# Attention and two gated layers on one core: the sixth head pair's reciprocals taken from the summed rows on VectorE, and two chunks' scores in one TensorE visit in the first stretch

## The chip, the cores and the metric

The kernel runs on one core of one Trainium2 chip. The metric is the device time of the program in microseconds (us); the time of a kernel is the median of its runs. TensorE does the matmuls, VectorE, ScalarE and GpSimd the work between them, and SP issues most of the DMAs. In the rows the engines are PE, DVE, ACT and POOL.

## The reference

Attention over 4 batches, 12 heads, 448 positions and 64 columns a head, with capped scores, followed by two feed-forward layers over the 1792 tokens of 768 columns. All is float32.

```python
scores = scale * np.matmul(q, k.transpose(0, 1, 3, 2))
scores = cap * np.tanh(scores / cap)
attn = np.exp(scores - max); attn = attn / (sum(attn) + 1e-09)
x = np.matmul(attn, v)
h = np.maximum(np.maximum(x @ w1, x @ w2), x @ w3) @ w_out
out = (silu(h @ w_gate) * (h @ w_val)) @ moe2_w_out
```

The lines are shortened; the feed-forward weights come in as 64-bit floats and are made into 32-bit ones on the chip.

## The kernel before, in words

**Pairs and chunks.** Two heads make a pair, six pairs a batch; g counts the 24 pairs from 0, so that the sixth pair is g = 5. The keys of a pair are cut into four chunks; chunk n belongs to pair n // 4. The first three chunks of a pair hold 128 keys of either head, the fourth holds the last 64 keys of both. For a chunk, `scores(n)` makes the products of keys and queries in PSUM (for the first three chunks two matmuls of 64 rows side by side, three times over, since each factor is held in two parts), `tanhs(n)` and `exps(n)` are ScalarE's tanh and exp, and `values(n)` adds the chunk's products with the values. The cap bounds the scores, so the exponent needs no maximum from the data. For pairs g < 8 (`PLAIN`) the values and exponentials are plain float32; from g = 8 on `parts(n)` cuts the exponentials into two parts, `eh` on ScalarE and `el` on VectorE (L286).

**The sums.** The values stand in a tile of three columns of blocks: the first head's values, a block of ones, the second head's values. The matmul of the first head takes the first two blocks, that of the second head the last two. So the sum of the exponentials comes out along with the products, once on each of 64 rows: below the products for the first head, above them for the second.

**From the sums to x.** `take(g)` copies the two PSUM tiles to `o`: the first head's by VectorE, with one row of sums (65 rows), the second head's by ScalarE, with all 128 rows. `sums_out(g)` loads a row of sums of each head by DMA into 112 rows of 8 (`su`), `invert(g)` takes the reciprocals there, `inverse_out(g)` stores them to memory (`rd`), `spread(g)` loads them back on 64 rows for each head (`rb`). `finish(g)` multiplies `o` by `rb` into `xp` (two multiplies, L366), and makes the two parts of `x` (L368, L369). In the first stretch `finish` is GpSimd's, but the sixth pair's is VectorE's. The tile `xp` has one buffer (L361), `e`, which holds tanh and exp, four (L267), the PSUM of the scores two, one for even and one for odd chunks (L257). The sums' PSUM of the second head has one buffer; for the first head it alternates between two in the first stretch (L179).

**The order of the work.** Everything runs in the order in which it is written out, engine by engine. `slot(n)` lists the steps around chunk n, with c = n % 4. The first stretch is the loop over n from -6 to 31 (L783), with `alone` set: there are no feed-forward matmuls yet. In slot n it does the exp of chunk n+1, the scores of chunk n+3, the tanh of chunk n+2 and the products of chunk n. In c = 0 the pair before is taken, with the second head's copy behind the tanh. Between the slots stand steps that make the feed-forward weights into 32-bit floats: `one`, `clamp` and `two` on VectorE (L609 to L624), `four` on GpSimd (L627), and `split_next`, which cuts a weight into two parts with ScalarE and GpSimd (L639 to L642), behind slots 27 and 30. Behind the stretch `alone` is cleared (L796), and the later slots are woven with the matmuls of the first feed-forward layer (`ff1`, L699). Slots of that part already do two chunks' scores in one visit: in c = 1 the chunks n+3 and n+4, in c = 2 none.

**The sixth pair.** Its sums are taken in slot 24 and sent off in slot 25, its reciprocals follow in slot 28, `rb` is loaded in slot 29, and VectorE finishes it in slot 31, behind that slot's `parts(32)` and `prep_k(9)`, which makes `kh9` and `kl9`. The fifth pair's `finish` stands in slot 28 on GpSimd.

Of the kernel before, what the change touches and what calls it, by code (L numbers as in the profile page):

```python
# [9 lines left out]
F32 = mybir.dt.float32  # L10
# [113 lines left out]
def program(ctx, tc, tensors, shared, general):  # L124

    nc = tc.nc
# [5 lines left out]
    B, H, S, D = q.shape  # L132
    P = 128
# [3 lines left out]
    NK = DM // P  # L137
# [181 lines left out]
    def take(g, heads=(0, 1)):  # L319

        if 0 in heads:
            if g < PLAIN:
                o[g] = res.tile([P, 2, S], F32, tag="x", name=f"o{g}", bufs=2 * NK)
            else:
                o[g] = ring.tile([P, 2, S], F32, tag="o", name=f"o{g}")
        for j in heads:
            r = slice(0, D + 1 if j == 0 else P)
            src, dst = pv[g][j][r, :S], o[g][r, j]
            if alone and j == 0:
                nc.vector.tensor_copy(dst, src)  # L330
            else:
                nc.scalar.activation(dst, src, AF.Copy)
# [17 lines left out]
    def spread(g):  # L350
        if g < NP:
            rb[g] = res.tile([P, 2, S], F32, tag="x", name=f"rb{g}", bufs=2 * NK)[:, 0]
        else:
            rb[g] = ring.tile([P, S], F32, tag="rb", name=f"rb{g}", bufs=1)
        for j in range(2):
            nc.sync.dma_start(
                out=rb[g][j * D : (j + 1) * D], in_=rd[g % 2][j].partition_broadcast(D)
            )

    def finish(g, eng=None):  # L360
# [42 lines left out]
    def slot(n):  # L403
# [5 lines left out]
        def add(cost, fn, i, end, *args):  # L409
            if 0 <= i < end:  # L410
                steps.append((cost, lambda: fn(i, *args)))
# [18 lines left out]
                    add(0, inverse_out, n // 4 - 2, NPAIR)  # L430
        add(0, exps, n + 1, NG)
        add(0, parts, n + 1, NG)
        together = c == 3 and not alone

        def products(i):
            if 0 <= i < NG:
                values(i)

        ahead = [n + 3] if alone else [[n + 3], [n + 3, n + 4], [], [n + 3]][c]

        def next_scores():
            for i in ahead:
# [4 lines left out]

        if ahead:
            steps.append((len(ahead) + together, next_scores))
        for i in [n + 2] if alone else ahead:  # L450
            add(0, tanhs, i, NG)
        if c == 0 and alone:
            add(0, take, n // 4 - 1, NPAIR, (1,))
            add(0, finish, n // 4 - 3, NPAIR)
            add(0, invert, n // 4 - 2, NPAIR)
            if n // 4 - 2 == NP - 1:
                add(0, inverse_out, NP - 1, NPAIR)
        if alone and n == -6:
            add(0, prep_q, 0, NPAIR)
        if n == 4 * PLAIN - 3:  # L460
            add(0, prep_v, PLAIN, NPAIR)
        if c == 1:
            add(0, sums_out, n // 4 - 1, NPAIR)
            if alone and n // 4 - 2 != NP - 1:
                add(0, inverse_out, n // 4 - 2, NPAIR)
            else:
                add(0, spread, n // 4 - 2, NPAIR)
            add(0, prep_q, (n + 7) // 4, NPAIR)
        if c == 2:
            if n > -4:  # L470
                add(0, load_k, n // 4 + 3, NPAIR)
            if alone and n // 4 - 2 != NP - 1:
                add(0, spread, n // 4 - 2, NPAIR)
            if not alone:
                add(0, prep_k, (n + 6) // 4, NPAIR)
                add(0, invert, n // 4 - 1, NPAIR)
                add(0, finish, n // 4 - 2, NPAIR)
        if c == 3:
            if alone:
                add(0, prep_k, (n + 5) // 4, NPAIR)  # L480
                if n // 4 - 2 == NP - 1:
                    add(0, finish, NP - 1, NPAIR, nc.vector)
            if not alone:
                add(0, inverse_out, n // 4 - 1, NPAIR)
            add(0, load_q, n // 4 + 4, NPAIR)
# [271 lines left out]
    with tc.manual_schedule():  # L757
# [22 lines left out]
        else:  # L780
            load_v(0)
            left = 4 * 10
            for n in range(-6, 4 * NP + FIRST):  # L783
# [8 lines left out]
                    ones(1)  # L792
                if n in (4 * NP + 3, 4 * NP + 6):
                    split_next()
            tanhs(4 * NP + FIRST + 2)
        alone.clear()  # L796
        for b in range(B - 1):
            if general:
# [502 lines left out]
```

## Time and profile before

| | us |
|---|---|
| median of 3 runs | 1048.73 (1047.07 to 1049.38) |
| the profiled execution, its own time | 1047.95 |
| its span, first to last instruction | 1046.2 |
| TensorE busy | 1026.9 (98%) |
| VectorE busy | 812.7 (78%) |
| ScalarE busy | 534.6 (51%) |
| GpSimd busy | 614.4 (59%) |
| chain that ended last, on TensorE | 83% |

Busy times are sums over the instructions of an engine. Matmuls are pipelined, so a busy TensorE need not be at its peak. The chain that ended last is followed back from the last instruction, at each step to what released it. A wait is put down to the event that came last. All times in the rows are us from the start of the span.

### The profile page before, as it was taken

To read this page: it belongs to the slowest core of one execution; us is meant where nothing else is said; L and a number is where in the kernel's file an instruction comes from. 1 tells how busy PE (TensorE), PEld (TensorE's weight loads), DVE (VectorE), ACT (ScalarE), POOL (GpSimd) and SP (SyncE) were. 2 spreads that over 40 slices of the span, in tenths; PEclk is the share of its full clock that TensorE was granted. 3 is DMA by queue.
4 is the path that set the end of the run, shared out by engine and by line. 5 is a ranking of instruction groups with operands and counts; after the bars stand their busy time and mean duration, and the time that the engine had idled before them with its cause. 6 is when DMAs were issued, how large, how long until landed. Compare 5 with 4: busy or idle time off the path is not lost.

```text
span 1046.2 us, 15070 instructions
## 1 busy us (share of the span) xinstructions
PE 1026.9 (98%) x5348; PEld 912.8 (87%) x5348; DVE 812.7 (78%) x1076; ACT 534.6 (51%) x843; POOL 614.4 (59%) x524
## 2 busy tenths in 40 slices
PE   8999999999999999999999999999999999999997
PEld 5555877888888888999999999999999999999997
DVE  5898889879889787877366977888887777986763
ACT  6887777767677764344445533333333334643331
POOL 2479977599999999999311356556666662000000
PEclk9999999999999999999999999999999999999999
DMA  7866344424435323434322023445544338765311
GB/s 179 205 165 169 78 125 130 130 64 136 120 105 145 107 83 108 144 105 140 96 83 87 1 61 122 156 158 167 169 161 135 96 112 254 210 181 147 103 46 41
DMA packets 153653, 131.42 MB, mean 126 GB/s; under 512 B 71136, under 2 KB 144096, under 8 KB 153568
## 3 DMA queue, kind: packets, MB, share of 16 engines
q1 hardware_dynamic: 147552, 108.67, 35.4%
q0 software_dynamic: 4944, 21.46, 6.5%
q8 instruction: 44, 0.72, 0.3%
q10 hardware_dynamic: 1072, 0.23, 0.1%
q14 instruction: 41, 0.34, 0.1%
HBM read 98.70 MB, written 31.54 MB: 124 GB/s over the span
## 4 chain that ended last, share of the span: by engine, by line
PE 83%; DVE 6%; POOL 5%; DMA 3%; issue 2%; ACT 2%; SPq 0%; ACTq 0%; POOLq 0%; DVEq 0%
PE ps_g L1036 29%; PE ps_h L699 19%; PE ps_o L1174 15%; PE ps_y L699 8%; PE pv L311 7%; PE sc L262 4%; DVE el L286 2%; POOL ws L642 2%; DVE xp L366 1%; PE pq L228 1%; DMA rb<-rd 1%; DMA vp<-in_v_dram 1%; POOL w L627 1%; POOL xp L366 1%; PE pk L242 1%
## 5 line engine op out<-in xcount | busy, mean ns | idle before, releaser
L699 PE MATMUL ps_h<-x,ws 128*128 128x448 f32 x1296 | 279.9, 366 | 3.4 <-POOL ws L642 3.4
L699 PEld LDWEIGHTS ps_h<-x,ws 128*128 128x128 f32 x1296 | 240.5, 188 | 30.2 <-issue 7.8
L642 POOL TENSOR_TENSOR ws<-w,ws 128x384 fp32r<-128x384 f32 x144 | 184.2, 1288 | 13.3 <-ACT ws L639 5.4
L627 POOL TENSOR_TENSOR t<-t,raw 128x768 uint32<-128x768 uint32 x42 | 82.6, 1967 | 113.9 <-DVE raw L624 107.1
L286 DVE TENSOR_TENSOR el<-e,eh 128x896 fp32r<-128x896 f32 x64 | 92.9, 1452 | 28.9 <-ACT eh L285 27.6
L276 ACT ACTIVATE e<-e,four 128x896 f32<-128x896 f32 x96 | 99.6, 1037 | 0.8
L1036 PE MATMUL ps_g<-yo,o_S 128*128 128x448 f32 x432 | 93.5, 362 | 0.0
L268 ACT ACTIVATE e<-sc,four 128x896 f32<-128x896 f32 x96 | 85.5, 905 | 13.3 <-PE sc L262 11.9
L699 PE MATMUL ps_y<-ha,ws 128*128 128x448 f32 x432 | 87.5, 364 | 0.0
L699 PEld LDWEIGHTS ps_y<-ha,ws 128*128 128x128 f32 x432 | 81.0, 188 | 6.3
L1036 PEld LDWEIGHTS ps_g<-yo,o_S 128*128 128x128 f32 x432 | 81.0, 187 | 5.4
L613 ACT ACTIVATE t<-raw 128x768 f32<-128x768 f32 x50 | 45.1, 903 | 65.5 <-DMA raw<-in_moe_w_val_dram 31.2
L311 PE MATMUL pv<-eh,vs 128*128 128x448 f32 (+1 forms) x256 | 77.5, 373 | 0.0
L641 POOL TENSOR_SCALAR ws<-w 128x384 fp32r<-128x384 f32 x90 | 71.7, 797 | 0.4
L1036 PE MATMUL ps_g<-yo,o_A 128*128 128x448 f32 x324 | 70.3, 362 | 0.0
L1036 PEld LDWEIGHTS ps_g<-yo,o_A 128*128 128x128 f32 x324 | 60.7, 187 | 4.1
L627 POOL TENSOR_TENSOR w<-w,raw 128x768 uint32<-128x768 uint32 x18 | 35.6, 1975 | 43.8 <-DVE raw L624 43.8
L617 DVE TENSOR_SCALAR t<-t 128x768 f32<-128x768 f32 x42 | 41.3, 984 | 25.5 <-ACT t L613 25.3
L1060 ACT ACTIVATE ct<-ct 128x448 f32<-128x448 f32 x23 | 13.3, 579 | 86.9 <-DVE ct L1059 86.9
L285 ACT ACTIVATE eh<-e 128x896 fp32r<-128x896 f32 x64 | 55.1, 861 | 4.7 <-ACT e L276 1.9
L639 ACT ACTIVATE g_S<-gr 128x384 fp32r<-128x384 f32 x56 | 27.2, 519 | 46.6 <-DVE gr L1155 40.4
L621 DVE SCALAR_TENSOR_TENSOR t<-raw,t 128x768 uint32<-128x768 uint32 x42 | 50.0, 1190 | 0.3
(160 smaller groups left out, 2191.9 us busy)
## 6 DMA issues: line engine op xcount, KB each, us to landing
raw<-in_moe_w_dram POOLq DMA_DIRECT2D x15, 768.0 KB, 5.6
gr<-gd SPq DMA_DIRECT2D x25, 384.0 KB, 5.3
raw<-in_moe_w_out_dram POOLq DMA_DIRECT2D x12, 768.0 KB, 5.4
raw<-in_moe_w_gate_dram SPq DMA_DIRECT2D x12, 768.0 KB, 4.7
raw<-in_moe_w_val_dram SPq DMA_DIRECT2D x12, 768.0 KB, 4.9
rb<-rd SPq DMA_DIRECT2D x48, 112.0 KB, 2.9
h<-ht SPq DMA_DIRECT2D x24, 224.0 KB, 2.0
hr<-h SPq DMA_DIRECT2D x24, 224.0 KB, 2.8
```

Of the source, the lines that this page charges most:

```text
L268: nc.scalar.activation(ee[n][:, :w], ps[:, :w, :S], AF.Tanh, scale=qsc)
L276: nc.scalar.activation(t, t, AF.Exp, bias=ncap, scale=acap)
L285: nc.scalar.activation(hi, t, AF.Copy)
L286: nc.vector.tensor_sub(lo, t, f(hi))
L311: nc.tensor.matmul(pv[g][j][:, :S], a, m, start=c == 0 and x == 0, stop=c == 3 and x == len(ops) - 1,)
L621: nc.vector.scalar_tensor_tensor(t3, high, 0xC0000000, apart, op0=ALU.bitwise_and, op1=ALU.bitwise_or)
L627: nc.gpsimd.tensor_tensor(t, t, low, op=ALU.add)
L641: copier.tensor_scalar(hi, src, 1.0, 1.0, ALU.mult, ALU.mult)
L642: subtracter.tensor_tensor(lo, src, f(hi), op=ALU.subtract)
L699: nc.tensor.matmul(ps, a, m, start=kk == 0 and n == 0, stop=kk == NK - 1 and n == 2)
L1036: nc.tensor.matmul(ps, a[:, s0, k3], m[:, kk, s1], start=kk == 0 and j == 0, stop=kk == 2 and j == 2,)
L1174: nc.tensor.matmul(ps, a[k // 3][:, s0, k3], w[:, k, s1], start=k == 0 and j == 0, stop=k == NHALF - 1 and j == 2,)
```

## The change

Two things are done, both in `slot` and what it calls.

For the sixth pair the trip of the sums through memory is left out. The first head's copy takes all 128 rows. A new function, `invert_here`, has VectorE take the reciprocals of the sums where they stand on 64 rows, 448 columns wide, once for each head, and writes them to the rows at which the products stand. It is called in slot 26. `sums_out`, `invert`, `inverse_out` and `spread` are not called for this pair, and its `finish` moves from slot 31 to slot 30.

In the first stretch, scores and tanhs follow the order of the later slots: chunk n+3 in c = 0, chunks n+3 and n+4 in c = 1, none in c = 2, chunk n+3 in c = 3. A tanh stands in the slot of its scores. In c = 3 the products of chunk n follow directly on the scores, ahead of the key transposes. The lone tanh behind the loop goes.

```diff
@@ -324,7 +324,7 @@
             else:
                 o[g] = ring.tile([P, 2, S], F32, tag="o", name=f"o{g}")
         for j in heads:
-            r = slice(0, D + 1 if j == 0 else P)
+            r = slice(0, D + 1 if j == 0 and g != NP - 1 else P)
             src, dst = pv[g][j][r, :S], o[g][r, j]
             if alone and j == 0:
                 nc.vector.tensor_copy(dst, src)
@@ -355,6 +355,13 @@
         for j in range(2):
             nc.sync.dma_start(
                 out=rb[g][j * D : (j + 1) * D], in_=rd[g % 2][j].partition_broadcast(D)
+            )
+
+    def invert_here(g):
+        rb[g] = res.tile([P, 2, S], F32, tag="x", name=f"rb{g}", bufs=2 * NK)[:, 0]
+        for j in range(2):
+            nc.vector.reciprocal(
+                rb[g][j * D : (j + 1) * D], o[g][(1 - j) * D : (2 - j) * D, j]
             )
 
     def finish(g, eng=None):
@@ -430,13 +437,13 @@
                     add(0, inverse_out, n // 4 - 2, NPAIR)
         add(0, exps, n + 1, NG)
         add(0, parts, n + 1, NG)
-        together = c == 3 and not alone
+        together = c == 3
 
         def products(i):
             if 0 <= i < NG:
                 values(i)
 
-        ahead = [n + 3] if alone else [[n + 3], [n + 3, n + 4], [], [n + 3]][c]
+        ahead = [[n + 3], [n + 3, n + 4], [], [n + 3]][c]
 
         def next_scores():
             for i in ahead:
@@ -447,30 +454,34 @@
 
         if ahead:
             steps.append((len(ahead) + together, next_scores))
-        for i in [n + 2] if alone else ahead:
+        for i in ahead:
             add(0, tanhs, i, NG)
         if c == 0 and alone:
             add(0, take, n // 4 - 1, NPAIR, (1,))
             add(0, finish, n // 4 - 3, NPAIR)
-            add(0, invert, n // 4 - 2, NPAIR)
-            if n // 4 - 2 == NP - 1:
-                add(0, inverse_out, NP - 1, NPAIR)
+            if n // 4 - 2 != NP - 1:
+                add(0, invert, n // 4 - 2, NPAIR)
         if alone and n == -6:
             add(0, prep_q, 0, NPAIR)
         if n == 4 * PLAIN - 3:
             add(0, prep_v, PLAIN, NPAIR)
         if c == 1:
-            add(0, sums_out, n // 4 - 1, NPAIR)
-            if alone and n // 4 - 2 != NP - 1:
+            if n // 4 != NP:
+                add(0, sums_out, n // 4 - 1, NPAIR)
+            if not alone:
+                add(0, spread, n // 4 - 2, NPAIR)
+            elif n // 4 - 2 != NP - 1:
                 add(0, inverse_out, n // 4 - 2, NPAIR)
-            else:
-                add(0, spread, n // 4 - 2, NPAIR)
             add(0, prep_q, (n + 7) // 4, NPAIR)
         if c == 2:
             if n > -4:
                 add(0, load_k, n // 4 + 3, NPAIR)
             if alone and n // 4 - 2 != NP - 1:
                 add(0, spread, n // 4 - 2, NPAIR)
+            if n // 4 == NP:
+                add(0, invert_here, NP - 1, NPAIR)
+            if n // 4 - 2 == NP - 1:
+                add(0, finish, NP - 1, NPAIR, nc.vector)
             if not alone:
                 add(0, prep_k, (n + 6) // 4, NPAIR)
                 add(0, invert, n // 4 - 1, NPAIR)
@@ -478,8 +489,6 @@
         if c == 3:
             if alone:
                 add(0, prep_k, (n + 5) // 4, NPAIR)
-                if n // 4 - 2 == NP - 1:
-                    add(0, finish, NP - 1, NPAIR, nc.vector)
             if not alone:
                 add(0, inverse_out, n // 4 - 1, NPAIR)
             add(0, load_q, n // 4 + 4, NPAIR)
@@ -792,7 +801,6 @@
                     ones(1)
                 if n in (4 * NP + 3, 4 * NP + 6):
                     split_next()
-            tanhs(4 * NP + FIRST + 2)
         alone.clear()
         for b in range(B - 1):
             if general:
```

## Rows read from the trace of the kernel before

**Rows 1.** Busy time by stretches: stretch, its length, engines, clock, DMA share, GB/s.
```profile
core 0: us, PE busy (x) PEld busy (x) DVE busy (x) ACT busy (x) POOL busy (x), PEclk, DMA share, GB/s
80.00:90.00 10.00, 10.00 (x46) 5.11 (x45) 9.42 (x13) 9.32 (x14) 9.65 (x8) 1.00 0.76 213
...
100.00:110.00 10.00, 7.68 (x35) 5.92 (x36) 8.92 (x9) 3.15 (x5) 9.75 (x9) 0.83 0.51 127
```

**Rows 2.** The waits from 85 to 112 us: in total, times, longest.
```profile
PE ps_h L699 <- POOL ws L642: 2.6, 1, 2.6
DVE xp L366 <- POOL x L369: 2.2, 1, 2.2
```

**Rows 3.** The chain in order of time: start, us, what.
```profile
44.07 1.50 PE pv L311 x4
...
54.92 7.57 DMA vp<-in_v_dram
...
63.75 4.99 DMA rb<-rd
```

**Rows 4.** The timeline of GpSimd: start, us, operation, what ended the idle time.
```profile
68.83 2.34 POOL L366 TENSOR_TENSOR xp<-o,rb 64x448 f32<-64x448 f32 x2 [5.03 <-DMA rb<-rd]
...
90.97 3.21 POOL L366 TENSOR_TENSOR xp<-o,rb 64x448 f32<-64x448 f32 x2
...
96.54 1.93 POOL L627 TENSOR_TENSOR w<-w,raw 128x768 uint32<-128x768 uint32 x1
```

**Rows 5.** The timeline of VectorE around the sixth pair's finish.
```profile
90.10 1.87 DVE L286 TENSOR_TENSOR el<-e,eh 128x896 fp32r<-128x896 f32 x1 [0.33 <-ACT eh L285]
...
96.11 2.84 DVE L366 TENSOR_TENSOR xp<-o,rb 64x448 f32<-64x448 f32 x2 [2.21 <-POOL x L369]
98.99 2.00 DVE L368 TENSOR_SCALAR x<-xp 128x448 fp32r<-128x448 f32 x1
101.03 0.81 DVE L369 TENSOR_TENSOR x<-xp,x 128x448 fp32r<-128x448 f32 x1
...
101.87 1.78 DVE L286 TENSOR_TENSOR el<-e,eh 128x896 fp32r<-128x896 f32 x1
```

**Rows 6.** The tile xp from 85 to 105 us: duration ns min/median/max, starts.
```profile
L366 DVE TENSOR_TENSOR xp<-o,rb x2: 619/1406/2194, 96.1 to 96.8; 64x448 f32<-64x448 f32 x2
```

**Rows 7.** The timeline of TensorE around chunk 32's products.
```profile
96.64 0.36 PE L311 MATMUL pv<-el,vs 128*128 128x448 f32 x1
...
100.79 1.57 PE L699 MATMUL ps_h<-x,ws 128*128 128x448 f32 x4 [2.58 <-POOL ws L642]
```

**Rows 8.** The timeline of SP's queue: the sixth pair's sums.
```profile
79.61 1.21 SPq L337 DMA_DIRECT2D su<-o  x2
```

**Rows 9.** Groups by line and form, VectorE, first 100 us: busy, mean ns.
```profile
L330 DVE COPY o<-pv 65x448 f32<-65x448 f32 x7 | 4.3, 610 | 0.0
...
L345 DVE RECIPROCAL rs<-su 112x8 f32<-112x8 f32 x6 | 1.1, 189 | 0.0
...
L760 DVE RECIPROCAL four<-four 128x1 f32<-128x1 f32 x1 | 0.2, 164 | 0.1
```

**Rows 10.** The timeline of TensorE: where the visits of one group begin.
```profile
35.48 0.47 PE L262 MATMUL sc<-qh,kh 64*128 64x448 f32 x2
...
38.34 0.47 PE L262 MATMUL sc<-qh,kh 64*128 64x448 f32 x2
...
40.85 0.47 PE L262 MATMUL sc<-qh,kh 64*128 64x448 f32 x2
...
45.51 0.47 PE L262 MATMUL sc<-qh,kh 64*128 64x448 f32 x2
```

**Rows 11.** The timeline of ScalarE in a group.
```profile
43.34 0.55 ACT L332 ACTIVATE o<-pv 128x448 f32<-128x448 f32 x1 [0.56 <-PE pv L311]
43.77 1.13 ACT L276 ACTIVATE e<-e,four 128x896 f32<-128x896 f32 x1
44.80 0.62 ACT L268 ACTIVATE e<-sc,four 128x448 f32<-128x448 f32 x1
...
46.43 1.01 ACT L268 ACTIVATE e<-sc,four 128x896 f32<-128x896 f32 x1 [0.20 <-PE sc L262]
```

## The prediction

> **What bounds the kernel now.** I read the busy table by stretches first. From 80 to 90 us TensorE has no idle time and a full clock, VectorE is busy for 9.42 of the 10 us and GpSimd for 9.65; only when the first feed-forward work is woven in does TensorE lose time, with 7.68 us busy and a mean clock of 0.83 from 100 to 110 us [rows 1]. So the stretch that the change touches is full on three engines, and what it is worth is read at its end. The list of waits around that end gives TensorE 2.6 us for GpSimd's L642, and VectorE 2.2 us for GpSimd's L369, which is the last operation of the fifth pair's finish [rows 2].
>
> The chain in order of time shows who sets that end. It is on TensorE until some 46 us, then goes through DMAs on SP's queue (a `vp` load of 7.57 us, the third pair's `rb` load) [rows 3] and enters GpSimd, where the third pair's finish begins at 68.83 us after 5.03 us of waiting for `rb`, the fifth pair's at 90.97 us, and L627 at 96.54 us [rows 4]. It comes back to TensorE only at 100.79 us. **So TensorE could have arrived earlier at no gain.**
>
> **VectorE at that end.** The sixth pair's finish is four VectorE instructions: at 96.11 us (two multiplies, 2.84 us together), 98.99 us (2.00 us) and 101.03 us (0.81 us). Ahead of them, at 90.10 us, stands the subtraction that makes `el32` (1.87 us); behind them, at 101.87 us, the one that makes `el33` (1.78 us) [rows 5]. The finish starts when the fifth pair's finish on GpSimd lets go of `xp`, which has one buffer (L361): the wait of 2.21 us is put down to L369 [rows 2, 5]. It does not wait for `rb`. TensorE reads `el32` at 96.64 us, in the second matmul of chunk 32's products [rows 7].
>
> **The change, part by part.** (1) *Reciprocals in place.* Removed are five issues of SP: two `su` loads (1.21 us together [rows 8]), one `rd` store, two `rb` loads. Since the finish waits for `xp` and not for `rb`, that trip lies beside other work today, and its removal brings nothing on the path; SP's later issues move up a little, but no row shows an engine at this end waiting for them. Removed from VectorE is a reciprocal of 0.19 us; added are two of 64x448 in slot 26 [rows 9]. No row shows one so wide. The copy of 65x448 takes 0.61 us, a lower end; the narrow reciprocals (8 columns 189 ns, 1 column 164 ns) give 25 / 7 = 3.6 ns a column, so 1.76 us each by estimate, an upper end [rows 9]. I take 1.76, as those are rows of the same operation: 3.5 us for both. Behind the finish instead of ahead of it come `el32` and the keys `kh9` and `kl9` (part 2), more than 3 us, so VectorE still reaches the finish about 2 us before L369 ends: the reciprocals are hidden by that wait. If that cover were gone they would cost up to 3.5 us.
>
> The Trainium skill (VectorE: DVE Perf Modes, First, the fixed hardware budget) says that the reciprocal runs as an iterated divide with a repeat count of 8. An estimate from that page, eight cycles of its 0.96 GHz for each of 448 columns, is 3.7 us each, and the sum would then be some 2 us more, as VectorE would come late to the finish. The rows speak against it: their 3.6 ns a column is less than half of that.
>
> (2) *The finish one slot earlier*, slot 30 instead of 31. This is the part that I think decides. In slot 31 it stood behind `el32`, `kh9` and `kl9`; in slot 30 it stands ahead of all three, and still waits for L369, since GpSimd's order is the same: 96.11 us. Its four instructions then run beside the same GpSimd work as before (memsets, L627, a load's issue, L642), so I take the same lengths and the same end, 101.84 us. `el32` follows where `el33` stood and takes its 1.78 us: done at 101.87 + 1.78 = 103.65 us [rows 5]. TensorE's second matmul of chunk 32 moves from 96.64 to 103.65 us, by 7.01 us. The wait of 2.58 us for L642, over at 100.79 us, lies behind it in TensorE's order and is gone by then [rows 7]: 7.01 - 2.58 = **+4.4 us** at that point. Behind `el32` also wait `kh9` and `kl9`; chunk 36's scores, the next that read them, come after that point.
>
> Why the two multiplies take 2.84 us is worth a look: the shorter takes 0.62 us, the longer 2.19 us [rows 6], and the longer runs beside GpSimd's L627. The Trainium skill (SBUF — State Buffer, SBUF: two separate sides) says that a VectorE instruction with two SBUF inputs and a GpSimd instruction take turns at a shared pair of ports, each for its whole length. By that rule the stretched lengths stay as they are, and the sum with them; were they an accident of this execution, rival B would hold.
>
> (3) *Two chunks in one visit.* Now a group of four chunks takes TensorE 45.51 - 35.48 = 10.03 us [rows 10]. Merging saves a visit: the slot from 38.34 to 40.85 us (2.51 us) shrinks to its products alone, 1.50 us as in the chain [rows 3, 10], and three score passes (some 0.6 us by estimate from the spacing within a visit) join the slot ahead: 0.4 us gained, with perhaps 0.1 more in the slot where scores and products now follow directly. So 9.5 us. But two waits come in. `e` has four buffers (L267): chunk n+4's tanh, now ahead of chunk n's products, writes chunk n's buffer and must wait for them on TensorE. Queued behind it on ScalarE are two exps and a tanh. And the copy that takes the second head's sum out of PSUM stays behind the tanh in slot c=0, which is now that of chunk n+3 and waits for scores of the same slot; the second half of chunk 0's products writes that PSUM. The loop: from the end of chunk 1's products ScalarE does tanh, exp (half width), exp, tanh, exp, tanh (half width) and the copy: four wide ones at about 1.03 us from start to start, two of half width at 0.66, the copy 0.55, so 6.0 us [rows 11]; then TensorE does half of chunk 0's products (0.8 us), two chunks' scores and the transposes (1.9 us by estimate) and chunk 1's products (1.7 us with the change of shape): 10.4, and some 0.1 of handing over: **10.5 us a group**. The stretch does not get shorter: seven groups by 0.5 us bring TensorE to chunk 32's products 3.5 us later, near 100 us. That is hidden by the wait to 103.65 us; without it, it costs 3.5 us.
>
> GpSimd's start at 68.83 us I take as unmoved: it comes from SP's DMAs [rows 3, 4], and SP is behind TensorE by more than the 2 us that four groups lose. All other edits (the test around the old reciprocal, the last tanh, the wider copy of the first head) are order without cost, hidden by the same waits.
>
> **The sum.** +4.4 us, with 0 for (1) and (3). Behind that point VectorE and TensorE are both nearly full again, so I see nothing that gives it back. The clock that fell after the idle 2.58 us (0.83 over ten us, so 1.7 us lost [rows 1]) I expect to fall once again, a little later, for the same price. The profiled execution took 1047.95 us, 0.78 us below the median of 1048.73 us: 1047.95 + 4.4 = 1052.3, and on the median **1053.1 us**. This forecast's own range is 1051 to 1055 us. A measurement of this kernel can tell 0.2%, 2.1 us, from no change.
>
> **Rivals.** *A, faster.* TensorE's visits set the pace, the copy does not hold them up, and GpSimd's head at 68.83 us moves up with them: eight groups by 0.5 us are 4.0 us: 1044.7 us. For it: TensorE shows no gap up to 90 us. Against it: the chain is on SP and GpSimd from 50 us on, and the two new waits close a loop. It decides if the third pair's `rb` lands before 66 us. Chance 0.13. *B, no change.* The finish runs at its shortest lengths, 0.62 + 0.62 + 0.61 (as the copy) + 0.81 = 2.7 us, and `el32` is done at 96.11 + 2.7 + 1.78 = 100.6 us. The wait for L642 still goes: 100.6 - 96.64 - 2.58 = +1.4 us, and with hardly an idle moment the clock does not fall, 1.7 us back: 1048.4 us. Against it: L627 and L642 stand on GpSimd right behind. Chance 0.15. *C, slower still.* VectorE comes late to the finish, by reciprocals longer than 1.76 us or by key tiles that TensorE turns later, and each us late adds one; with 2.4 us, 1055.5 us. Chance 0.14. *D*, that the change does not do what it says, is in the forecast: the trip through memory goes away, but nobody waited for it. The forecast has 0.58.
>
> **The numbers.** Below 1046.6 us: A and a little of B, 0.16. Within 2.1 us: the rest of B and a tail of the forecast, 0.14. Above 1050.8 us: 0.70. The range leaves out A and the end of C: 1047.0 to 1056.5 us.
>
> **What would show it.** Right: VectorE waits some 2 us for L369 with `el32` behind the finish; TensorE's longest wait is for L286 at chunk 32, some 3 to 4 us, and the one for L642 is gone; groups take 10.5 us. Wrong: TensorE is through chunk 32's products before 101 us; the fifth pair's finish ends on GpSimd well before 95 us; groups take 9.5 us; reciprocals take over 2 us each.

## The result, and the profile after

The changed kernel takes **1054.37 us** (median of 5 runs, 1053.34 to 1059.64) against 1048.67 us for the kernel before on the same chip: a ratio of **1.0067, interval 1.0053 to 1.0081**, so slower by 5.6 to 8.5 us (the two medians differ by 5.70 us). The forecast was 1053.1 us with a range of 1047.0 to 1056.5 us. The profiled execution has a span of 1052.3 us against 1046.2 us, 6.1 us more. In the code printed above, which is the kernel before, lines count from its own top; the changed kernel's stand 7 to 9 lines further down behind the new function (L366 is L373 there, L369 is L376, L627 is L636, L642 is L651), and `invert_here` is L363.

The same busy table of stretches as in [rows 1], for the changed kernel:

```profile
80.00:90.00 10.00, 5.49 (x24) 2.61 (x22) 9.91 (x7) 6.56 (x9) 8.19 (x8) 0.96 0.59 159
90.00:100.00 10.00, 9.49 (x34) 5.09 (x34) 6.46 (x11) 4.40 (x6) 9.19 (x9) 0.70 0.41 93
```

Before, TensorE was busy for all of 80 to 90 us. Now it is busy for 5.49 us of it, and the next ten run at a mean clock of 0.70. VectorE is full from 80 to 90 us, but with only 7 instructions, where it had 13. Two of them are the long reciprocals, as its timeline shows (start, us, operation, what ended the idle time):

```profile
82.79 5.92 DVE L363 RECIPROCAL rb<-o 64x448 f32<-64x448 f32 x2
...
89.62 0.68 DVE L220 CAST kh<-pk 128x512 fp32r<-128x512 f32 x1
...
98.17 0.69 DVE L211 TENSOR_TENSOR vs<-vn,vs 128x512 fp32r<-128x512 f32 x1 [3.43 <-ACT vs L210]
...
99.97 1.65 DVE L373 TENSOR_TENSOR xp<-o,rb 64x448 f32<-64x448 f32 x2
...
103.63 2.15 DVE L286 TENSOR_TENSOR el<-e,eh 128x896 fp32r<-128x896 f32 x1
```

This answers to [rows 5]. The two reciprocals take 5.92 us, 2.96 us each, where 1.76 was taken. The finish does not wait for GpSimd any more: it starts at 99.97 us, behind `vs` (the values in two parts) and the queries `qh9` and `ql9`, 3.9 us later than before. It then needs only 3.66 us up to `el32` (103.63 - 99.97), where the finish of [rows 5] had needed 5.7. `el32` is made from 103.63 us on.

TensorE, same columns:

```profile
90.35 0.74 PE L262 MATMUL sc<-qh,kh 64*128 64x448 f32 x2 [3.37 <-DVE kh L220]
...
105.84 0.47 PE L311 MATMUL pv<-el,vs 128*128 128x448 f32 x1 [1.84 <-DVE el L286]
...
115.44 0.60 PE L228 MATMUL pq<-ident,qn 112*128 112x112 f32 x4 [1.53 <-ACT e L268]
```

TensorE waits 3.37 us for keys that VectorE makes behind the reciprocals, and 1.84 us for `el32`. The read of `el32` moved from 96.64 us [rows 7] to 105.84 us, by 9.20 us; the wait of 2.58 us for L642 is gone: 9.20 - 2.58 = 6.6 us. The third row is a useful **mark** for all that follows: the transposes of the next pair's queries, which in every kernel here begin after a wait of 1.53 or 1.54 us for ScalarE's L268. Before it stood at

```profile
108.94 0.60 PE L228 MATMUL pq<-ident,qn 112*128 112x112 f32 x4 [1.53 <-ACT e L268]
```

so it moved by 6.50 us, and the span grew by 6.1. (The two executions start alike: GpSimd's first L627, which is L636 in the changed kernel, begins at 22.54 us in both.) The loss is made by then, and hardly any of it is given back.

### The profile page after: what moved, and what is told of

It is laid out like the page before. It is cut to its first block, busy times and chain, and to the rows that moved or that the text cites. A ratio compares the mean times of both kernels' runs of the same rounds, so it can differ in the third digit from the quotient of the medians.

```text
span 1052.3 us, 15098 instructions
## 1 busy us (share of the span) xinstructions
PE 1024.4 (97%) x5348; PEld 914.9 (87%) x5348; DVE 818.1 (78%) x1077; ACT 530.5 (50%) x843; POOL 613.8 (58%) x524
## 4 chain that ended last, share of the span: by engine, by line
PE 81%; DVE 10%; ACT 3%; issue 2%; POOL 2%; DMA 1%; ACTq 0%; SPq 0%; POOLq 0%; DVEq 0%
PE ps_g L1044 29%; PE ps_h L708 19%; PE ps_o L1182 15%; PE ps_y L708 8%; PE pv L311 6%; PE sc L262 4%; DVE el L286 2%; POOL ws L651 1%; ACT e L268 1%; DVE xp L373 1%; ACT e L276 1%; PE pq L228 1%; DVE w L630 1%; DVE raw L633 1%; DVE w L626 1%
## 5 line engine op out<-in xcount | busy, mean ns | idle before, releaser
L651 POOL TENSOR_TENSOR ws<-w,ws 128x384 fp32r<-128x384 f32 x144 | 182.2, 1274 | 19.5 <-ACT ws L648 11.7
L636 POOL TENSOR_TENSOR t<-t,raw 128x768 uint32<-128x768 uint32 x42 | 82.7, 1969 | 114.1 <-DVE raw L633 104.5
L286 DVE TENSOR_TENSOR el<-e,eh 128x896 fp32r<-128x896 f32 x64 | 92.3, 1443 | 28.5 <-ACT eh L285 27.2
L268 ACT ACTIVATE e<-sc,four 128x896 f32<-128x896 f32 x96 | 85.3, 905 | 30.7 <-PE pv L311 15.5
L636 POOL TENSOR_TENSOR w<-w,raw 128x768 uint32<-128x768 uint32 x18 | 35.3, 1963 | 43.7 <-DVE raw L633 43.7
L311 PE MATMUL pv<-e,vp 128*128 128x448 f32 (+1 forms) x128 | 49.1, 556 | 5.6 <-ACT o L332 4.1
```

The source lines that it names most:

```text
L268: nc.scalar.activation(ee[n][:, :w], ps[:, :w, :S], AF.Tanh, scale=qsc)
L286: nc.vector.tensor_sub(lo, t, f(hi))
L311: nc.tensor.matmul(pv[g][j][:, :S], a, m, start=c == 0 and x == 0, stop=c == 3 and x == len(ops) - 1,)
L636: nc.gpsimd.tensor_tensor(t, t, low, op=ALU.add)
L651: subtracter.tensor_tensor(lo, src, f(hi), op=ALU.subtract)
```

## The experiments

Theory T: the finish ahead of `el32` is the loss, the reciprocals delay the keys on top of it, and the merged visits are nearly free. Each expectation below says what T means for its run. All runs in one table; the ratio is to the kernel before on the same chip, the mark is in us from the start of each kernel's profiled span, and the last column counts it from the key transposes (L242) of slot 23, ahead of everything in which kernels with the same visits differ.

| kernel | edit to the kernel before | ratio (interval) | mark | mark from slot 23 |
|---|---|---|---|---|
| before | | 1 | 108.94 | 37.2 |
| changed | all three | 1.0067 (1.0053 to 1.0081) | 115.44 | 43.2 |
| e1 | finish in slot 30 | 1.0048 (1.0031 to 1.0065) | 114.93 | 42.0 |
| e2 | merged visits | 1.0016 (1.0002 to 1.0029) | 107.40 | 33.4 |
| e3 | reciprocals in place | 1.0021 (1.0010 to 1.0031) | 111.23 | 38.5 |
| e4 | visits, finish in slot 30 | 1.0048 (1.0030 to 1.0065) | 113.41 | 40.4 |
| e12 | reciprocals, finish in slot 30 | 1.0040 (1.0026 to 1.0054) | 111.99 | 39.3 |
| e8 | reciprocals, behind the keys | 1.0030 (1.0017 to 1.0043) | 110.65 | 39.6 |
| e9 | as e3, copies for reciprocals | 0.9998 (0.9989 to 1.0007) | 109.97 | 37.2 |
| e10 | changed, copies for reciprocals | 1.0042 (1.0028 to 1.0055) | 115.18 | 41.1 |
| e5 | second weight split behind slot 28 | 0.9993 (0.9982 to 1.0004) | 104.43 | 32.8 |
| e6 | visits, second head's copy ahead of the exp | 0.9987 (0.9977 to 0.9996) | 108.40 | 37.0 |
| e7 | e5 and e6 | **0.9976** (0.9962 to 0.9989) | 105.42 | 35.4 |
| e11 | e7 and reciprocals in place | 1.0026 (1.0015 to 1.0037) | 111.50 | 42.5 |

The starts of the profiled executions differ by up to 2.5 us (GpSimd's first L627 begins between 22.20 and 24.65 us), so two marks are best compared through the last column, and that only where the visits are the same: before, e1, e3, e12, e8, e9 and e5; changed, e2, e4 and e10; e6, e7 and e11. What a kernel is worth, the ratios tell.

### The three parts one by one: e1, e2, e3

e1 moves only the finish:

```diff
+            if alone and n // 4 - 2 == NP - 1:
+                add(0, finish, NP - 1, NPAIR, nc.vector)
             if not alone:
                 add(0, prep_k, (n + 6) // 4, NPAIR)
...
-                if n // 4 - 2 == NP - 1:
-                    add(0, finish, NP - 1, NPAIR, nc.vector)
```

> The kernel before with one part of the change alone: the sixth pair's finish in slot 30 instead of slot 31, ahead of el32, kh9 and kl9 on VectorE; the trip through memory and the old visits stay. Theory T (the prediction's part 2): the finish still starts when GpSimd's L369 lets go of xp, near 96 us, el32 is done near 103.6 us, TensorE waits for it at chunk 32, and the kernel takes 4.4 us more, 1052 to 1054 us. Theory U (the whole loss comes from the reciprocals and the visits, the place of the finish is free): within 1 us of before.

Measured: 1.0048, 5.0 us of 1046.93. Its VectorE and TensorE timelines:

```profile
96.99 2.81 DVE L366 TENSOR_TENSOR xp<-o,rb 64x448 f32<-64x448 f32 x2 [4.52 <-POOL x L369]
...
102.62 1.88 DVE L286 TENSOR_TENSOR el<-e,eh 128x896 fp32r<-128x896 f32 x1
```

```profile
104.55 0.74 PE L311 MATMUL pv<-el,vs 128*128 128x448 f32 x1 [6.49 <-DVE el L286]
```

This is the prediction's part 2 as it was written: VectorE stands idle for 4.52 us until GpSimd lets go of `xp`, the finish takes its stretched 5.6 us, `el32` comes behind it, and TensorE waits 6.49 us for it. Counted from slot 23, the mark is 4.7 us later.

e2 merges only the visits:

```diff
-        together = c == 3 and not alone
+        together = c == 3
...
-        ahead = [n + 3] if alone else [[n + 3], [n + 3, n + 4], [], [n + 3]][c]
+        ahead = [[n + 3], [n + 3, n + 4], [], [n + 3]][c]
...
-        for i in [n + 2] if alone else ahead:
+        for i in ahead:
...
-            tanhs(4 * NP + FIRST + 2)
```

> The kernel before with the merged visits alone; trip through memory and finish in slot 31 stay. Theory T: groups of 10.2 us with a wait of 0.7 us for the second head's copy in each; TensorE reaches the end of the stretch some 1 us later, which comes out of its wait of 2.6 us for L642: within 1.5 us of before. Theory U: the waits for the copy, seven by 0.7 us, are the loss: 4 to 6 us slower.

Measured: 1.0016, an interval that almost reaches no change. TensorE reads `el32` at 99.47 us and the wait for L642 is gone, as the prediction had it ("near 100 us", hidden by that wait). The 1.7 us, a little over T's 1.5, was not traced to a place: the mark is earlier than before, not later. That lead is gone two pairs later (the same transposes at 149.98 us against 149.86), as TensorE waits 3.2 us for VectorE's `el` between 109 and 152 us where it had waited 1.6.

e3 takes only the reciprocals in place, with the finish left in slot 31:

```diff
+            if n // 4 == NP:
+                add(0, invert_here, NP - 1, NPAIR)
             if not alone:
                 add(0, prep_k, (n + 6) // 4, NPAIR)
```

with the lines of the change that leave out the pair's trip through memory.

> The kernel before with the sixth pair's reciprocals in place alone (slot 26); finish in slot 31, old visits. Theory T: the two reciprocals take 5.9 us together and hold up the keys kh8 and kl8, which VectorE makes next: in the run before these were ready 1.4 us ahead of TensorE in slot 29, now TensorE waits some 4 us there; the wait of 2.6 us for L642 shrinks by as much: 1.5 to 4 us slower. Theory U: VectorE's work is hidden, as the prediction had it: within 1 us of before.

Measured: 1.0021, and the mark 1.2 us later, counted from slot 23. Its VectorE and TensorE timelines:

```profile
82.74 5.93 DVE L363 RECIPROCAL rb<-o 64x448 f32<-64x448 f32 x2
```

```profile
90.31 0.47 PE L262 MATMUL sc<-qh,kh 64*128 64x448 f32 x2 [3.58 <-DVE kh L220]
```

The wait for the keys is there with this part alone, so it comes from the reciprocals and from nothing else in the change.

### Two parts together: e4 and e12

e4 is e1 and e2 together.

> The changed kernel with the sixth pair's trip through memory put back (sums, reciprocals and broadcast by DMA), its visits and its finish in slot 30 kept. Theory T (reciprocals and place of the finish both matter, and overlap): no wait for kh8, the finish waits for GpSimd near 96 us, el32 near 102 to 103.6 us: 3 to 5 us slower than before, some 2 us faster than the changed kernel. Rival (the reciprocals alone are the loss): as before within 1 us.

Measured: 1.0048, as e1. In this kernel the merged visits add nothing to the finish's loss. But the finish does not wait for GpSimd, as T had it. Its VectorE timeline:

```profile
92.47 0.93 DVE L211 TENSOR_TENSOR vs<-vn,vs 128x512 fp32r<-128x512 f32 x1 [3.37 <-ACT vs L210]
...
96.14 2.39 DVE L366 TENSOR_TENSOR xp<-o,rb 64x448 f32<-64x448 f32 x2 [1.54 <-DMA rb<-rd]
```

The wait ahead of the finish is put down to the load of `rb`: with the merged visits and the finish in slot 30, VectorE does wait for the trip through memory. And VectorE waits 3.37 us for `vs`, as in the changed kernel, without any reciprocal ahead of it.

e12 is the changed kernel without the merged visits, run after e9 to e11 below.

```diff
-        together = c == 3
+        together = c == 3 and not alone
...
-        ahead = [[n + 3], [n + 3, n + 4], [], [n + 3]][c]
+        ahead = [n + 3] if alone else [[n + 3], [n + 3, n + 4], [], [n + 3]][c]
...
-        for i in ahead:
+        for i in [n + 2] if alone else ahead:
...
+            tanhs(4 * NP + FIRST + 2)
```

> The changed kernel without its second part in the first stretch: reciprocals in place in slot 26 and the finish in slot 30, but one chunk's scores a visit and the tanhs as before. Theory T (in the changed kernel the reciprocals hold up the keys by 3.4 us, and on top of that the merged order puts a tanh that waits for TensorE ahead of the cast of vs on ScalarE, so VectorE waits 3.4 us for vs and starts the finish at 99.97 us instead of some 97): without the merged visits VectorE has vs in time (waits under 1 us for L210), starts the finish at 96 to 98 us, the finish takes its stretched 5.7 us again, el32 is read by TensorE at 104 to 105.5 us instead of 105.84, ratio 1.0053 (1.004 to 1.0065). Rival U (the merged visits have nothing to do with it; the delay of the keys alone makes vs late): VectorE waits 3 us or more for L210 here too, el32 is read at 105.8 us, ratio 1.0067.

Measured: 1.0040, the lower end of T's range. The places are T's but for the finish's length, which is 4.9 us instead of 5.7. Its VectorE and TensorE timelines:

```profile
95.37 0.68 DVE L211 TENSOR_TENSOR vs<-vn,vs 128x512 fp32r<-128x512 f32 x1
...
97.16 1.74 DVE L373 TENSOR_TENSOR xp<-o,rb 64x448 f32<-64x448 f32 x2
```

```profile
91.07 0.47 PE L262 MATMUL sc<-qh,kh 64*128 64x448 f32 x2 [4.46 <-DVE kh L220]
...
104.05 0.36 PE L311 MATMUL pv<-el,vs 128*128 128x448 f32 x1
```

TensorE waits for the keys and then not at all for `el32`, which VectorE has done at 103.55 us, before TensorE comes to it. So with the old visits the two delays do not add; e12 (1.0040) is no slower than the finish alone (e1, 1.0048).

VectorE does not wait for `vs` here. The reason is on ScalarE: the cast that `vs` is made from, first in e12, then in the changed kernel:

```profile
86.40 0.62 ACT L210 ACTIVATE vs<-vn 128x512 fp32r<-128x512 f32 x1
```

```profile
96.61 1.01 ACT L268 ACTIVATE e<-sc,four 128x896 f32<-128x896 f32 x1 [3.72 <-PE pv L311]
97.52 0.62 ACT L210 ACTIVATE vs<-vn 128x512 fp32r<-128x512 f32 x1
```

In the merged order a tanh stands ahead of that cast, and it waits 3.72 us for products of TensorE that free its `e` buffer. Those products are themselves late, because TensorE had waited for the keys. VectorE's wait for `vs` comes from the merged order alone (3.37 us in e4, 3.43 us in the changed kernel); but in e4 it is over at 92.47 us, before `rb` is there, and in the changed kernel only at 98.17 us. So there the merged visits are not free: they pass the reciprocals' delay on to `vs`, and through VectorE's order to the finish and to `el32`, read at 105.84 us, after a wait of 1.84 us, instead of 104.05 without one. The ratios agree, 1.0067 against 1.0040; their intervals just touch, and the difference is some 0.7 to 4.9 us, an estimate that takes the errors of the two as independent.

### Is it the length of the reciprocals, or their place? e8, e9, e10

e8 puts them one slot later, behind the keys:

```diff
                 add(0, prep_k, (n + 5) // 4, NPAIR)
+                if n // 4 == NP:
+                    add(0, invert_here, NP - 1, NPAIR)
```

> The kernel before with the sixth pair's reciprocals in place as in e3, but one slot later, behind the key tiles kh8 and kl8 that TensorE needs in slot 29; finish in slot 31. Theory T (their cost in e3 is the lateness of those keys, not VectorE's time as such): TensorE no longer waits in slot 29, el32 comes up to 1 us late: within 1.5 us of before, at least 1 us faster than e3. Rival (VectorE is full, so 5.9 us cost the same anywhere): as e3, 2 us or more slower than before.

**T's expectation fell.** Measured: 1.0030, no better than e3. Its VectorE and TensorE timelines:

```profile
83.68 0.69 DVE L247 TENSOR_TENSOR kl<-pk,kh 128x512 fp32r<-128x512 f32 x1
84.40 5.93 DVE L363 RECIPROCAL rb<-o 64x448 f32<-64x448 f32 x2
...
95.33 0.63 DVE L235 TENSOR_TENSOR ql<-pq,qh 128x448 fp32r<-128x448 f32 x1
```

```profile
96.06 1.08 PE L242 MATMUL pk<-ident,kn 128*128 128x128 f32 x4 [4.84 <-issue]
```

The keys are in time, and TensorE stops 4.84 us at the next thing: the key transposes. The row names no releaser; the wait ends just when VectorE is done with `ql9` (95.33 + 0.63 = 95.96 us), and in the code the transposes of queries and keys share one PSUM tile (`tr`) in the first stretch, so I read it as that tile being held until then. In e10 and e11 below the same nameless wait ends 0.11 us behind `ql9` too (at 97.59 and 98.31 us). This is argued from the code and the times and was not tried by itself. In both places tried, VectorE had no free 5.9 us, and moving the reciprocals only changed which of its debts TensorE waited for.

e9 and e10 leave the order as it is and shorten the two instructions: a copy of the same 64x448 in place of each reciprocal, in e3 and in the changed kernel, which leaves out the division by the sums.

```diff
-            nc.vector.reciprocal(
+            nc.vector.tensor_copy(
```

> The kernel before with the sixth pair's reciprocals in place (slot 26, finish left in slot 31), as in the run with this part alone (ratio 1.0021), but with each of the two 64x448 reciprocals replaced by a VectorE copy of the same 64x448 elements. The sixth pair of the first batch is so multiplied by its sums instead of divided by them; no other work differs. Theory T (the loss of this part is the duration of the two reciprocals, 2.96 us each, which hold up the keys): two copies of some 0.6 us each leave 4.7 us of VectorE free, TensorE no longer waits 3.6 us for the keys at 90 us, the wait of some 2.6 us for L642 is back, and the ratio is 1.000 (0.999 to 1.001). Rival U (the loss comes from the missing trip and the new order, not from the length of the two instructions): 1.002 as with the reciprocals.

> The changed kernel with each of the two 64x448 reciprocals replaced by a VectorE copy of the same size; the sixth pair of the first batch is so multiplied by its sums instead of divided by them. Theory T: VectorE again reaches the finish ahead of L376 and waits for it, the finish in slot 30 still stands ahead of el32, so what remains of the loss is that of the finish in slot 30: ratio 1.0045 (1.003 to 1.006), with TensorE waiting 4 to 6 us for el32 and hardly for the keys. Rival U (the reciprocals cost nothing beside the finish, the whole loss is the order): 1.0067 as the changed kernel.

e9 measured 0.9998: T. The two copies took 1.88 us together, the wait for the keys is gone, and L651 is waited for again, as L642 was before (2.6 us there). Its VectorE timeline and the list of its waits from 85 to 120 us:

```profile
82.78 1.88 DVE L363 COPY rb<-o 64x448 f32<-64x448 f32 x2
```

```profile
PE ps_h L708 <- POOL ws L651: 2.5, 1, 2.5
DVE xp L373 <- POOL x L376: 1.6, 1, 1.6
```

So with the old visits leaving out the trip through memory is worth nothing that these runs can tell, and the loss of e3 is the length of the reciprocals.

e10 measured 1.0042 as T expected (1.0045). Its VectorE and TensorE timelines:

```profile
97.97 2.86 DVE L373 TENSOR_TENSOR xp<-o,rb 64x448 f32<-64x448 f32 x2 [0.49 <-POOL x L376]
...
103.64 1.89 DVE L286 TENSOR_TENSOR el<-e,eh 128x896 fp32r<-128x896 f32 x1
```

```profile
105.59 0.47 PE L311 MATMUL pv<-el,vs 128*128 128x448 f32 x1 [4.16 <-DVE el L286]
```

At first sight the reciprocals cost nothing beside the finish: `el32` is started at 103.64 us here and at 103.63 in the changed kernel. But this execution is 1.82 us behind the other one long before the two kernels differ, as the key transposes of slot 23 show, first in the changed kernel, then in e10:

```profile
72.29 0.65 PE L242 MATMUL pk<-ident,kn 128*128 128x128 f32 x4
```

```profile
74.11 0.66 PE L242 MATMUL pk<-ident,kn 128*128 128x128 f32 x4
```

Counted from there, the copies bring the finish forward by 3.8 us, it is 2.0 us longer, and `el32` is read 2.1 us earlier (105.84 - 105.59 + 1.82), as is the mark (41.1 against 43.2 us). The ratios differ by 0.0025, some 0.6 to 4.7 us by the same kind of estimate as for e12. **So in the merged order the reciprocals cost 2 to 2.6 us on top of the finish**, about what they cost alone (e3, 2.2 us), and e4, with the trip in their place, points the same way, though its ratio's difference lies within the errors (1.0048, mark 40.4). With the old visits they cost nothing on top of it (e12 against e1). The traces put the difference down to the order on ScalarE: in the merged one `vs`, and the finish behind it, come after the products that the late keys hold up.

### What held the time before: e5, e6, e7, e11

e5 puts the second split of a weight behind slot 28 instead of slot 30, so that L642 is done sooner:

```diff
-                if n in (4 * NP + 3, 4 * NP + 6):
+                if n in (4 * NP + 3, 4 * NP + 4):
```

> The kernel before, with the second split of a weight (ScalarE L639, GpSimd L641 and L642) put behind slot 28 instead of slot 30, so that on GpSimd it stands ahead of the last conversion L627 and the load issued behind it. Theory T (GpSimd's order sets the end of the first stretch): L642 for the second group is done some 3 us earlier, near 97.6 us, TensorE's wait of 2.6 us goes and its clock does not fall: 2.5 to 4.5 us faster than before. Rival (the wait is taken over by another, el33 or the sixth pair's x, at the same place): within 1 us of before.

Measured: 0.9993, no change; the expectation for the whole time missed, though the place did what it should. The wait for L642 is gone, and TensorE's full clock stays: the mark is at 104.43 us, 4.51 us earlier. The rows behind it:

```profile
104.43 0.60 PE L228 MATMUL pq<-ident,qn 112*128 112x112 f32 x4 [1.53 <-ACT e L268]
119.10 0.47 PE L311 MATMUL pv<-el,vs 128*128 128x448 f32 x1 [1.55 <-DVE el L286]
...
133.98 0.47 PE L311 MATMUL pv<-el,vs 64*128 64x448 f32 x1 [1.71 <-DVE el L286]
```

At the same transposes of the two pairs behind it the lead over the kernel before is 2.69 us (125.43 against 128.12) and 1.15 us (148.71 against 149.86). So it is given back within 45 us: 1.55 us to a new wait for VectorE's `el` at 119.10 us, and most of the rest around the wait at 133.98 us, where the clock from 132 to 138 us is 0.72 (1.00 before). VectorE's `el` is what TensorE waits for next.

e6 merges the visits and takes the copy that held them up out of the way, ahead of the exp:

```diff
                 add(0, take, n // 4 - 1, NPAIR, (0,))
+                add(0, take, n // 4 - 1, NPAIR, (1,))
...
-            add(0, take, n // 4 - 1, NPAIR, (1,))
             add(0, finish, n // 4 - 3, NPAIR)
```

> The kernel before with the merged visits, and the second head's copy out of PSUM put ahead of the exp in slot c=0. Theory T: the wait of 0.7 us for the copy goes, a group takes 9.5 us instead of 10.2, TensorE reaches the end of the stretch some 4 us earlier than before and waits there for L642, 5 us or more, with its clock falling as before: no gain, within 1.5 us of before. Rival A of the prediction (TensorE's visits set the pace and GpSimd's work moves up with them): 3 to 5 us faster than before. Another rival (the loop over the four buffers of e holds a group at 10 us without the copy): groups of 10 us, as before.

Measured: 0.9987, and groups of 9.2 to 9.7 us. The list of its waits from 20 to 64 us has no wait of TensorE for the copy, and TensorE spends most of the gain on waiting for GpSimd, in its timeline:

```profile
100.29 1.33 PE L699 MATMUL ps_h<-x,ws 128*128 128x448 f32 x4 [3.95 <-POOL ws L642]
```

e7 is both edits.

> The two edits of e5 and e6 together: merged visits with the copy first, second split behind slot 28. Theory T: TensorE comes early, GpSimd's L642 is done near 97 us, so the gain is about that of e5 and perhaps 1 us more, as GpSimd and VectorE are full up to there: 3 to 5 us faster than before. Rival A: both gains add up, 6 to 8 us faster.

Measured: 0.9976, the fastest kernel here, faster than both the kernel before and the changed one: 1045.38 us against 1046.73 us by medians, 1.2 to 4.0 us by the interval. T's 3 to 5 us did not come, nor rival A's 6 to 8. At the transposes of the two pairs behind the mark e7 is still 2.70 and 2.66 us ahead of the kernel before (125.42 and 147.20 us), though its execution began 0.75 us later. e6 alone runs into the wait for L642 that e5 takes away, and e5's lead went to VectorE's `el`; but the intervals of e6 and e7 overlap, so that e7 is faster than e6 is not shown.

e11 adds the reciprocals in place to e7, with the finish in slot 31.

> The change with three repairs: the finish of the sixth pair back in slot 31 behind el32, the second head's copy ahead of the exp in c=0, and the second weight split behind slot 28 instead of 30. It is the fastest kernel so far (ratio 0.9976) with the in-place reciprocals added. Theory T (VectorE is full in this stretch, so two reciprocals of 2.96 us cost TensorE 2 to 4 us wherever they stand): 1.0005 (0.9995 to 1.002), TensorE waiting 3 us or more for keys made behind the reciprocals. Rival U (once the order is mended, leaving out the trip through memory is free or a gain): 0.9976 or below.

Measured: 1.0026. The sign is T's, the size is not: 1.0005 was expected, with an upper end of 1.002. Its TensorE timeline and its busy table:

```profile
87.85 0.74 PE L262 MATMUL sc<-qh,kh 64*128 64x448 f32 x2 [5.14 <-DVE kh L220]
...
98.31 1.03 PE L242 MATMUL pk<-ident,kn 128*128 128x128 f32 x4 [1.90 <-issue]
```

```profile
80.00:90.00 10.00, 4.32 (x19) 2.39 (x17) 9.84 (x8) 4.27 (x7) 9.37 (x9) 0.74 0.51 129
90.00:100.00 10.00, 8.08 (x33) 4.72 (x30) 7.42 (x9) 7.20 (x10) 9.39 (x10) 0.84 0.40 99
```

TensorE, earlier by e7's gain, only waits longer for the keys, and the clock falls behind the wait. The mark of e11 (111.50) lies with those of e3, e8 and e12 (111.23, 110.65, 111.99), whose starts differ by up to 1.4 us: with 5.9 us more on VectorE, the mark is at some 110.7 to 112 us whether the visits, the split, the copy or the finish are moved or not. Among the kernels with the reciprocals only the changed one, with all three parts, is later still.

## Why the prediction was right, and where it was not

**The direction and its reason were right.** Part 2 had +4.4 us; alone it measures +5.0 us (e1; 4.7 us at the mark), by the mechanism named: `el32` behind a finish that waits for GpSimd, the wait for L642 gone. That TensorE could arrive earlier at no gain is what e6 shows (its wait for L642 grew to 3.95 us).

**The mis-sized term is in part 1**: the reciprocal was taken at 1.76 us, "an upper end", and measures 2.95 us, so both take 5.92 us from start to end and not 3.5. The slope was drawn from instructions of 8 columns and of 1, where most of the time does not go with the columns (188 - 8 x 6.3 = 138 ns). From 8 columns (188 ns) to 448 columns (2947 ns) it is (2947 - 188) / 440 = 6.3 ns a column, where 3.6 was taken; an upper end drawn from two nearly equal short lengths bounds nothing. These are the groups of VectorE's instructions by line and form, the first 104 us of the changed kernel:

```profile
L363 DVE RECIPROCAL rb<-o 64x448 f32<-64x448 f32 x2 | 5.9, 2947 | 0.1
...
L345 DVE RECIPROCAL rs<-su 112x8 f32<-112x8 f32 x5 | 0.9, 188 | 0.0
```

The Trainium skill (VectorE: DVE Perf Modes, First, the fixed hardware budget) gives the reciprocal a repeat count of 8, from which the prediction had estimated 3.7 us. The measured 2.95 us lies between the rows' 1.76 and that, and the estimate from the page was the nearer by 0.4 us.

**The claim that the reciprocals are hidden failed**, and not only by their length. The cover that I named was VectorE's wait for L369, at the finish. But between slot 26 and the finish VectorE owes TensorE the keys, and TensorE waited 3.37 us for those (3.58 in e3) long before the cover came. I had asked what the reciprocals push at the end of the road and not what stands next behind them on the engine. VectorE then came late to the finish: this is the mechanism of rival C, and it joined the forecast's instead of replacing it. The term of the sum that failed is thus the 0 for part 1: the reciprocals cost 2.2 us alone (e3) and 2 to 2.6 us in the changed kernel (against e10).

**The finish's length was taken as fixed** at 5.7 us, with rival B for a short one. It is 5.6 us in e1 and 3.66 us in the changed kernel, where it begins behind GpSimd's L636 instead of beside it; its two multiplies took 2.84 us together [rows 5, 6] and take 1.65 now. The rows of GpSimd's timeline in the changed kernel:

```profile
96.19 1.83 POOL L636 TENSOR_TENSOR w<-w,raw 128x768 uint32<-128x768 uint32 x1
98.42 0.83 POOL L564 DMA_DIRECT2D raw<-in_moe_w_dram  x1 [0.41 <-POOL w L636]
99.29 1.01 POOL L651 TENSOR_TENSOR ws<-w,ws 128x384 fp32r<-128x384 f32 x1
```

The Trainium skill (SBUF — State Buffer, SBUF: two separate sides) says that such VectorE and GpSimd instructions take turns at a shared pair of ports. These rows agree as far as they go: no GpSimd L636 beside the multiplies, no stretch of 2.19 us. What the late start cost, 3.9 us, the shorter finish gave back by 2.0 us, and that is why the forecast was missed by so little: `el32` was read 105.84 - 103.65 = 2.2 us later than predicted. This is luck: a start and a length were both wrong, and the errors had opposite signs.

**Part 3 was right in its mechanism and nearly in size**: 10.2 us a group measured (35.20 to 45.39 us) against 10.5, and 10.03 before [rows 10]. The two waits it named are there. TensorE's timeline, and ScalarE's total from the list of waits, first 84 us:

```profile
44.44 1.02 PE L311 MATMUL pv<-e,vp 128*128 128x448 f32 x2 [0.69 <-ACT o L332]
45.39 0.47 PE L262 MATMUL sc<-qh,kh 64*128 64x448 f32 x2
```

```profile
ACT e L268 <- PE pv L311: 11.8, 7, 1.7
```

Its price of 0 held with the finish alone (e4 against e1) and failed beside the reciprocals (changed against e12), where the same `e` buffer wait held up the cast of `vs`.

**The rivals.** A wanted shorter groups. They came only where the copy was moved ahead of the exp (e6), and even there the time fell by only 0.13%, since GpSimd sets the end. B had the finish at its shortest lengths, and C a VectorE that comes late. The changed kernel has something of both, and they work against each other. D, the trip for which nobody waited, is what e9 shows; in the merged order with the finish in slot 30 it would have been waited for (e4, 1.54 us).

**The clock.** I expected it to fall once more for the same price, behind the one wait. It fell behind the wait for the keys, earlier and for longer: 0.70 from 90 to 100 us.

Of the signs that the prediction listed, the missing wait for L642 and the order of `el32` behind the finish came; the wait of 2 us for L369 and TensorE's 3 to 4 us for L286 did not (0 and 1.84 us), as both had turned into the wait for the keys and for `vs`. "Reciprocals take over 2 us each" was among the signs of wrong, and it was the one that came.

## What to carry to other kernels

Before adding work to an engine that is full, list what that engine owes to others between the new work and the place where you think it is hidden: the first of these that another engine waits for sets the price, and in e8 moving the work only changed which one it was. Take the length of an instruction from rows that differ in the dimension that you scale, by at least as much as you scale it. Price a part in the order in which it will stand: the same reciprocals cost 2.2 us alone, nothing on top of the finish in the old order of visits and 2 to 2.6 us on top of it in the merged one. Before you compare a time in two traces, find work ahead of the edit and subtract what lies between the starts: here 1.82 us of it hid the price of the reciprocals. And where one early engine meets two waits in a row, take both away in one kernel, as e7 did, before you call either edit worthless.

## What the runs showed of the hardware that I had not expected

A VectorE reciprocal of float32 costs 6.3 ns a column, so that 64x448 takes 2.95 us (2946 to 2948 ns in the changed kernel and in e3), where two copies of the same shape took 0.64 and 1.21 us (e9). It uses 64 of the 128 rows for that time; the same sums spread over 112 rows of 8 columns take 0.19 us, and that is what the trip through memory had been buying.

TensorE's clock fell behind each of the longer waits of these traces, from the 2.5 us of e9 (0.72 from 102 to 108 us) to the 6.49 us of e1 (0.58 in the same stretch). In the changed kernel it was 0.50 from 90 to 96 us, after 1.74 us of busy time in the six us before, and full again from 96 us on:

```profile
84.00:90.00 6.00, 1.74 (x4) 0.68 (x4) 5.94 (x4) 2.56 (x4) 4.64 (x5) 0.93 0.30 82
90.00:96.00 6.00, 5.65 (x20) 3.57 (x21) 4.67 (x7) 1.01 (x1) 5.63 (x6) 0.50 0.34 78
96.00:102.00 6.00, 5.69 (x27) 3.32 (x26) 3.73 (x6) 5.36 (x7) 5.47 (x6) 1.00 0.66 151
```

In that stretch 0.50 is the lower of its two levels, 1.2 of 2.4 GHz: a pair of score matmuls takes 0.58 us there, in the timeline, and 0.36 us at the full clock, and such pairs start 0.37 and 0.20 us apart. So the wait of 3.37 us was followed by 5.65 us of busy time at half the clock, which is some 2.6 to 2.8 us more than at the full one, an estimate from these rows.
